# An attention and feed-forward kernel on one core: GpSimd ordered behind VectorE by semaphores, one more batch in 64-row bursts, and a new order of work

## The chip, the cores and the metric

The kernel runs on one core of a Trainium2 chip. The metric is the device time in microseconds (us) of one execution. The kernel before took 301.77 us in the median of three runs (301.6 to 303.27).

A core has five engines with a queue of instructions each: TensorE (PE in the profile) for matrix products, VectorE (DVE), ScalarE (ACT), GpSimd (POOL), and SyncE (SP), which here only issues transfers. TensorE writes its products to PSUM, eight banks of 128 partitions by 512 fp32 numbers. VectorE and ScalarE read PSUM and SBUF; GpSimd here works on SBUF alone. An engine works its queue in order, and waits for another engine by a semaphore.

## What is computed

```python
B, H, S, D, M = 8, 8, 576, 64, 128          # batch, heads, tokens, head size, features
q_s, k_s = q * D**-0.25, k * D**-0.25
phi(x) = exp(x @ omega.T - |x|^2/2 - rowmax) / sqrt(M)
kv = sum_s phi(k)[s, m] * v[s, d]           # per batch and head: 128 x 64
z  = sum_s phi(k)[s, m]
attn = (phi(q) @ kv) / (phi(q) @ z + 1e-6)
x = attn, heads side by side                # 4608 tokens x 512
h = x @ w_in                                # 512 x 2048
g = h * clip(h + 3, 0, 6) / 6
out = g @ w_out                             # 2048 x 512, fp32 out
```

Factors that are the same in numerator and denominator drop out, so that the kernel needs of `phi(q)` only an exponential, and of `phi(k)` an exponential divided by its row's maximum (`mx`, and its reciprocal `cc`), which is multiplied into v (`vc`).

## The kernel before

**Stages.** Attention is done batch by batch (0 to 7), and one stage behind it the feed-forward part block by block: 512 tokens of a batch are a block, and the 64 tokens left over of each of the eight batches form the ninth (block 8). In a stage of some 30 us the engines share the attention of batch b, the first product (`mm1`) of block b-1 and the second product (`P0` to `P6`) of block b-2.

**Attention.** The rows of q and k come in transposed (`kT`, `qT`), 18 chunks of 128 columns that hold two 64-row halves each. They are projected on omega (`burst`, or `e_K` at line 840 and `project` at line 860). Batches 0 to 2 use the second way: a matmul of 128 rows and 256 columns for each of 18 k chunks, and two matmuls of 512 columns for each four q chunks, where half of omega's rows are zeros. Batches 3 to 7 use bursts (`ROWS = 3`): four bursts, `R.0` with six chunks and `R.1` to `R.3` with four each, in which the two 64-row halves of the array work side by side (lines 796 and 799). A burst of four chunks fills four PSUM banks, and `R.0` six, at once. ScalarE takes the exponential of each bank (lines 815, 824, or 847, 864), VectorE the maximum (820 or 851). For each of four pairs of heads (`pair`), `vc` (line 970; GpSimd, or eight small ScalarE instructions at 972) and `vcc` (977, 978) scale v, `vcl` (886, 889) does so for the left-over tokens, then TensorE forms `kv` (986, 988) and `num` (1014), and VectorE divides (`rec`, `div`; 1026, 1030). A transposing transfer from SP's queue brings the result to `xT`.

**Feed-forward.** The first product is plain (`mm1`, line 1083) or, for half of the columns from block 2 on and all of them from block 7 on, in seven products instead of eight (`mm1_quad`, line 1248): its sums of weights and inputs (`W`, `X1` to `X4`) are made at line 1343, and it holds four banks X, Y, Z, W. In a quad, `q3` copies W to the SBUF tile `p7`, and `q5` (line 1276) adds Z and `p7` back into bank W, which stays taken until the two instructions of the activation, `qr2` on ScalarE and `qg2` on VectorE (1284, 1286), have read it. The second product of blocks 1 to 8 is in seven products as well (`P0` to `P6`, line 1415); its sums `S1` to `S4` over the activations are again made by `combine` at line 1343, by GpSimd or VectorE.

**What sets the order.** `ORDER` lists every operation by its number, engine by engine; these lists are the order in each queue, and decide which engine does what. `schedule` runs through them with costs written beside each operation (its `occ`, `lat`, `issue`), only to give out PSUM banks and to note which operation must wait for which; `emit` writes the instructions and semaphore waits. Operations with a `port` (GpSimd's arithmetic, and VectorE's `combine` and `vc`) are kept apart in that model by `shared`, but no wait is written for it.

```python
                if e in o.port:
                    shared[0] = o.end - (0.07 if e == "POOL" else 0.0)
```

Loads: batch 0 comes as fp32 by SP and ScalarE; later q and k are cast on the way by GpSimd's queue, and v comes by SP's. From batch 3 on the loads wait for marks in the first product (`("m1", b - 2, 2)` and so on).

Of the kernel before, what the change touches and what calls it, by code (L numbers as in the profile page):

```python
# [16 lines left out]
EV0 = (("ACT","DVE"), ("ACT","DVE"), ("POOL", "ACT"), {"k": ("POOL", "ACT", "DVE"), "q": ("POOL", "ACT","DVE")})  # L17
# [4 lines left out]
        14, 121, 115, 117, 131, 138, 159, 147, 119, 141, 150, 144, 156, 135, 127, 153, 123, 125, 176, 129, 133, 174,  # L22
        166, 170, 172, 168, 188, 190, 203, 162, 178, 205, 164, 218, 193, 180, 220, 233, 208, 195, 235, 210, 407, 248,
        395, 223, 401, 198, 396, 238, 402, 397, 240, 408, 403, 398, 245, 225, 409, 404, 410, 213, 413, 416, 243, 228,
        271, 419, 291, 251, 422, 425, 428, 431, 275, 281, 434, 277, 437, 279, 318, 440, 443, 273, 309, 446, 315, 306,
        289, 285, 449, 312, 287, 297, 300, 586, 596, 303, 326, 320, 597, 336, 576, 294, 587, 330, 577, 588, 328, 283,
        578, 598, 332, 324, 589, 322, 599, 357, 579, 566, 359, 567, 362, 344, 580, 590, 568, 346, 334, 383, 569, 570,
        571, 349, 370, 385, 591, 365, 572, 581, 375, 372, 388, 600, 601, 592, 582, 583, 352, 391, 593, 573, 378, 602,
        603, 617, 505, 620, 614, 623, 466, 469, 475, 478, 635, 490, 472, 629, 632, 487, 481, 647, 484, 659, 644, 507,
        501, 653, 638, 497, 493, 668, 503, 499, 665, 662, 495, 650, 779, 511, 509, 531, 519, 780, 521, 536, 533, 524,  # L30
        789, 555, 782, 783, 560, 557, 790, 543, 712, 545, 548, 792, 793, 692, 795, 798, 799, 705, 796, 816, 810, 813,
        719, 819, 825, 828, 840, 831, 834, 845, 842, 844, 802, 863, 847, 803, 868, 849, 851, 865, 744, 870, 867, 732,
        987, 874, 737, 997, 734, 988, 872, 768, 756, 746, 1003, 749, 761, 990, 758, 998, 773, 770, 991, 1000, 1001, 900,
        1004, 1006, 1007, 913, 1018, 1024, 1021, 920, 1010, 1027, 1033, 927, 1039, 1050, 1048, 1036, 1011, 1042, 1053,
        1071, 1052, 1073, 1055, 1076, 1057, 1075, 952, 1059, 1078, 1080, 1195, 940, 976, 1082, 942, 957, 1196, 945, 954,
        1205, 964, 1198, 969, 966, 1199, 1206, 978, 981, 1121, 1208, 1209, 1108, 1214, 1215, 1128, 1229, 1232, 1226,
        1241, 1135, 1235, 1244, 1256, 1247, 1250, 1261, 1258, 1260, 1211, 1263, 1279, 1212, 1265, 1284, 1267, 1283,
        1281, 1218, 1286, 1403, 1404, 1290, 1148, 1160, 1219, 1150, 1165, 1288, 1184, 1162, 1153, 1406, 1413, 1414,
        1329, 1189, 1407, 1186, 1172, 1416, 1174, 1177, 1336, 1417, 1419, 1420, 1316, 1422, 1423, 1440, 1437, 1434,
        1452, 1464, 1449, 1443, 1466, 1468, 1469, 1458, 1455, 1471, 1426, 1473, 1427, 1343, 1475, 1487, 1356, 1611,  # L40
        1491, 1492, 1358, 1380, 1489, 1361, 1494, 1382, 1368, 1612, 1370, 1498, 1496, 1373, 1614, 1392, 1621, 1615,
        1622, 1537, 1394, 1397, 1385, 1624, 1625, 1544, 1627, 1628, 1551, 1630, 1634, 1631, 1524, 1635, 1642, 1645,
        1672, 1648, 1651, 1657, 1660, 1677, 1674, 1676, 1663, 1564, 1576, 1679, 1566, 1578, 1569, 1666, 1681, 1695,
        1581, 1683, 1588, 1699, 1600, 1590, 1697, 1593, 1700, 1722, 1702, 1602, 1723, 1605, 1704, 1706, 1753, 1732,
        1725, 1776, 1726, 1733, 1757, 1758, 1755, 1781, 1735, 1760, 1736, 1762, 1764, 1778, 1780, 1783, 1741, 1799,
        1742, 1787, 1785, 1738, 1804, 1801, 1824, 1803, 1806, 1822, 1739, 1808, 1810, 1826, 1827, 1745, 1876, 1829,
        1746, 1831, 1833, 1878, 1845, 1881, 1880, 1901, 1846, 1883, 1899, 1885, 1848, 1904, 1903, 1849, 1887, 1924,
        1906, 1922, 1908, 1855, 1927, 1926, 1856, 1910, 1929, 1945, 1858, 1931, 1949, 1933, 1950, 1859, 1861, 1947,
        1862, 1952, 1864, 1978, 1865, 1956, 1968, 1969, 1868, 1869, 1954, 1979, 1984, 1971, 1981, 1982, 1985, 1972,
        1988, 1989, 1997, 2003, 2000,  # L50
    ],
    "SP": [
        0, 18, 22, 33, 20, 23, 26, 25, 24, 27, 28, 32, 29, 30, 31, 262, 260, 261, 465, 464, 462, 463, 461, 459, 460,
# [72 lines left out]
        1390, 1462, 1485, 1619, 1463, 1509, 1640, 1638, 1641, 1560, 1575, 1559, 1574, 1562, 1654, 1402, 1587, 1586,  # L126
        1598, 1656, 1655, 1669, 1692, 1670, 1749, 1715, 1874, 1728, 1717, 1671, 1694, 1731, 1730, 1729, 1796, 1872,
        1797, 1873, 1819, 1875, 1774, 1844, 1821, 1843, 1896, 1898, 1851, 1897, 1775, 1919, 1853, 1852, 1921, 1854,
        1944, 1965, 1976,
    ],  # L130
}

# [288 lines left out]
def _emit(nc, es, q, k, v, omega, w_in, w_out, out):  # L421
# [803 lines left out]
    def mm1_quad(blk, f):  # L1225
# [11 lines left out]
        def bank(v):  # L1237
            return v.ring.t[v.slot]
# [373 lines left out]
```

## Time and profile before

| what | before |
|---|---|
| median of three runs | 301.77 us |
| the profiled execution | 302.46 us, span 300.6 us |
| TensorE busy | 292.2 us, 97% of the span, 2899 matmuls |
| VectorE busy | 271.4 us, 90% |
| ScalarE busy | 212.9 us, 71% |
| GpSimd busy | 206.3 us, 69% |
| granted TensorE clock | 1.000 |
| share of the last chain on TensorE | 81% |

The span runs from the first to the last instruction; the 1.86 us between it and the execution's time lie around it. A matmul's busy time overlaps the next one's, so that 97% is not a share of useful work: the distance from one start to the next is the measure. That distance is 109 ns for 256 columns and 216 ns for 512 whenever nothing is waited for. In the views, `L1415` and the like are lines of the kernel before, and `x8` counts merged instructions.

### The profile page before, as it was taken

What the parts mean: (1) busy time and instruction counts of PE and PEld (TensorE: products, weight loads), DVE (VectorE), ACT (ScalarE), POOL (GpSimd) and SP (SyncE); (2) the same over time, 40 slices, a digit from 0 to 9 for tenths busy, and PEclk for the clock granted to TensorE, in tenths of its full rate; (3) what the DMA queues carried; (4) which work ended last, traced back from release to release, by engine and by line L of the source; (5) the groups of instructions that cost most, each with busy time, mean ns of one, the idle gap of its engine ahead of it and who ended that gap; (6) DMA issues with size and microseconds to landing.
All of it is one profiled execution on the core that took longest, in us unless ns stands there. A gap on an engine that the chain in (4) does not pass through costs nothing.

```text
span 300.6 us, 7551 instructions
## 1 busy us (share of the span) xinstructions
PE 292.2 (97%) x2899; PEld 222.1 (74%) x2899; DVE 271.4 (90%) x593; ACT 212.9 (71%) x479; POOL 206.3 (69%) x226
## 2 busy tenths in 40 slices
PE   7999999999999999999989999999999999999996
PEld 5688955554884798569736887588757788888885
DVE  4889898889999998999879998999999999997875
ACT  2975899199878992997587776985887576687310
POOL 1664827039898986589939869998279939869711
PEclk9999999999999999999999999999999999999999
DMA  7999999999999997799769898999531600300034
GB/s 234 292 188 168 266 200 127 197 215 155 242 110 234 126 191 138 173 139 196 171 169 172 144 241 129 106 200 220 86 94 57 166 0 3 126 16 0 2 143 140
DMA packets 90100, 44.90 MB, mean 149 GB/s; under 512 B 57936, under 2 KB 87760, under 8 KB 90064
## 3 DMA queue, kind: packets, MB, share of 16 engines
q1 hardware_dynamic: 62064, 30.71, 46.1%
q0 software_dynamic: 26592, 12.46, 33.7%
q10 hardware_dynamic: 1408, 1.25, 1.3%
q8 instruction: 23, 0.38, 0.5%
q14 instruction: 13, 0.11, 0.1%
HBM read 36.73 MB, written 9.44 MB: 154 GB/s over the span
## 4 chain that ended last, share of the span: by engine, by line
PE 81%; DVE 8%; ACT 5%; POOL 5%; issue 1%; POOLq 0%
PE p L1415 29%; PE p L1248 15%; PE p L1083 11%; PE p L1327 5%; PE p L1302 4%; PE p L1014 3%; PE p L986 2%; DVE mx L820 2%; PE p L796 2%; POOL s L1343 2%; PE p L597 2%; ACT kp L847 2%; PE p L860 2%; POOL vc L970 1%; PE p L840 1%; PE p L799 1%
## 5 line engine op out<-in xcount | busy, mean ns | idle before, releaser
L1284 ACT ACTIVATE tsb<-p 128x512 f16<-128x512 f32 x72 | 41.4, 601 | 21.8 <-PE p L1248 12.0
L1083 PE MATMUL p<-xT,wi 128*128 128x512 f16 x224 | 53.1, 379 | 1.8 <-ACT qpT L824 1.4
L1286 DVE SCALAR_TENSOR_TENSOR gT<-tsb,p 128x512 f16<-128x512 f16 x72 | 46.8, 676 | 3.0 <-ACT tsb L1284 2.8
L1415 PE MATMUL p<-wo,gT 128*128 128x256 f16 x368 | 47.0, 273 | 0.0
L1083 PEld LDWEIGHTS p<-xT,wi 128*128 128x128 f16 x224 | 21.3, 98 | 24.9 <-ACT qpT L824 2.1
L1091 DVE SCALAR_TENSOR_TENSOR gT<-tsb,p 128x512 f16<-128x512 f16 x56 | 36.4, 674 | 3.1 <-ACT tsb L1089 2.8
L1415 PEld LDWEIGHTS p<-wo,gT 128*128 128x128 f16 x368 | 34.8, 98 | 4.9 <-issue 0.5
L1089 ACT ACTIVATE tsb<-p 128x512 f16<-128x512 f32 x56 | 33.2, 620 | 7.0 <-PE p L1083 5.3
L543 ACT COPY p<-p 128x512 f32<-128x512 f32 x55 | 32.2, 599 | 4.1 <-PE p L1415 2.0
L970 POOL TENSOR_TENSOR vc<-v,cc 128x512 bf16<-128x512 f32 x27 | 28.7, 1061 | 7.1 <-DVE cc L964 5.2
L824 ACT ACTIVATE qpT<-p 128x512 bf16<-128x512 f32 (+1 forms) x50 | 27.7, 577 | 6.8 <-PE p L799 6.8
L1343 POOL TENSOR_TENSOR gT<-gT,s 128x512 f16<-128x512 f16 x21 | 24.3, 1157 | 12.0 <-PE p L1415 10.6
L1415 PE MATMUL p<-t,gT 128*128 128x256 f16 x256 | 31.8, 273 | 0.4 <-DVE u L1431 0.4
L1343 POOL TENSOR_TENSOR gT<-gT 128x512 f16<-128x512 f16 x24 | 28.2, 1177 | 4.7 <-DVE s L1343 3.2
L815 ACT ACTIVATE kp<-p 128x512 bf16<-128x512 f32 (+1 forms) x50 | 26.8, 571 | 5.9 <-PE p L799 5.6
L820 DVE TENSOR_REDUCE mx<-kp 128x4 f32<-128x512 bf16 (+1 forms) x50 | 29.3, 618 | 0.3 <-ACT kp L815 0.3
L643 POOL DMA_DIRECT2D kb<-in_k_dram x21 | 16.2, 774 | 18.8 <-PE p L1083 18.1
L1030 DVE TENSOR_TENSOR xb<-p,rec 128x384 f16<-128x384 f32 (+1 forms) x64 | 28.2, 467 | 0.3
L1415 PEld LDWEIGHTS p<-t,gT 128*128 128x128 f16 x256 | 24.3, 98 | 5.4 <-issue 1.3
L1343 POOL TENSOR_TENSOR s<-gT,s 128x512 f16<-128x512 f16 x21 | 24.4, 1164 | 3.4 <-DVE s L1343 2.2
L1343 POOL TENSOR_TENSOR s<-gT 128x512 f16<-128x512 f16 x19 | 22.0, 1158 | 4.7 <-DVE gT L1286 3.1
L643 POOL DMA_DIRECT2D qb<-in_q_dram x28 | 19.6, 713 | 7.5 <-PE p L1083 5.0
(139 smaller groups left out, 671.4 us busy)
## 6 DMA issues: line engine op xcount, KB each, us to landing
v<-in_v_dram SPq DMA_DIRECT2D x14, 512.0 KB, 4.8
out_dram<-osb SPq DMA_DIRECT2D x14, 512.0 KB, 3.3
kb<-in_k_dram POOLq DMA_DIRECT2D x14, 256.0 KB, 5.0
qb<-in_q_dram POOLq DMA_DIRECT2D x14, 256.0 KB, 5.6
wo<-in_moe_w_out_dram POOLq DMA_DIRECT2D x8, 256.0 KB, 9.9
wi<-in_moe_w_in_dram POOLq DMA_DIRECT2D x3, 512.0 KB, 7.5
q<-in_q_dram SPq DMA_DIRECT2D x4, 256.0 KB, 4.8
vl<-in_v_dram SPq DMA_DIRECT2D x8, 128.0 KB, 4.2
```

The source lines that it names most:

```text
L543: return E.copy(dst(), src())
L643: lambda E: E.dma_start(dst, src), prio + 0.001 * turn_of[0], reads=gate, writes=keys,
L820: op("DVE", dvet(128 * (d1 - d0)), lambda E, ko=ko, mo=mo: E.reduce_max(mo, ko, axis=AX.X), p0 + 0.01, reads=[("kp", 0, d, lh) for d in ra ...
L970: return E.tensor_tensor(vcm[:, :, 0:D], v32[:, m, :, :], cbc, ALU.mult)
L1083: ins = E.matmul(ring.t[vh.slot], wi[:, c, 128 * f:128 * f + 128], xv[:, c, :], start=(c == 0), stop=(c == NJ - 1))
L1089: op("ACT", actt(512), lambda E: E.activation(tsb[tu][:], ring.t[vh.slot], AF.Relu, bias=0.5, scale=1.0 / 6.0), t - 0.1, reads=[vh], write ...
L1091: op("DVE", dvet(512), lambda E: E.scalar_tensor_tensor(gT[gu][:, f, :], tsb[tu][:], 1.0, ring.t[vh.slot], ALU.min, ALU.mult), t - 0.1, re ...
L1248: ins = E.matmul(bank(v)[:, 256 * g:256 * g + 256], w(c, f + g), x[:, c, :], start=start and g == 0 and c == 0, stop=c == 1, skip_group_ch ...
L1284: op("ACT", actt(512), lambda E, v=v, tu=tu: E.activation(tsb[tu][:], bank(v), AF.Relu, bias=0.5, scale=1.0 / 6.0), t - 0.1, reads=[v], wr ...
L1286: op("DVE", dvet(512), lambda E, v=v, tu=tu, dst=dst: E.scalar_tensor_tensor(dst, pieces(tsb[tu][:]), 1.0, pieces(bank(v)), ALU.min, ALU.m ...
L1343: op(engines, {"POOL": 0.1 + n / 475.0, "DVE": 0.09 + n / 2000.0}, lambda E: E.tensor_tensor(dst, x, y, ALU.subtract if minus else ALU.add ...
L1415: ins = E.matmul(ring.t[v.slot][:, 256 * j:256 * j + 256], a[:, f, 128 * j:128 * j + 128], w[:, f, :], start=(first and f == 0 and j == 0) ...
```

## The change

Three things are done together, and all five lists of `ORDER` are new.

1. **GpSimd waits for VectorE.** `schedule` remembers the last VectorE operation with a `port` (`holder`), and lets each following `port` operation of GpSimd depend on it, if by the model less than 4 us lie between. `emit` makes a semaphore wait of it where no other wait covers it. `qg2` of each quad joins these VectorE operations, since `q5` now writes its sum to `p7` in SBUF in place of bank W: `qr2` and `qg2` then read SBUF, and bank W is free once `q3` has copied it.
2. **Bursts from batch 2.** `ROWS` goes from 3 to 2: the third batch's 9 `K` and 10 `Q` operations become `R2.0` to `R2.3`.
3. **A new sequence.** TensorE's queue has 546 operations for 561, ScalarE's 456 for 442, VectorE's 592 for 593, GpSimd's 215 for 222; SP's 112 for 112. `vc` of batch 0 is cut in two halves by v's two loads. Loads from batch 3 on have no marks to wait for. Many costs in the model are other numbers; they emit nothing, and act only through bank choice and through `holder`.

By names, the parts of the lists that matter below: `vc.0.1` is `vc` of batch 0, pair 1, and a second operation of one name has a mark ('); `wi` and `wo` are loads of the weights, `kl.1` and `k10.1` loads of batch 1, `Tevk` and `Tevq` copies of transposed k and q out of PSUM, `eK` and `eQ` the exponentials. GpSimd at the start, before: `wi1 wi0 wi0' wi2 vcl.0 vc.0.0 vc.0.1 vcc.0.2 vc.0.2 vc.0.3 kl.1 wi3 k00.1`; after: `wi1 wi0 wi0' vc.0.0 vc.0.0' vcl.0' vcl.0 vc.0.1' wi2 wi3 kl.1 vcc.0.3 k10.1`. ScalarE between `eK0.6` and its first `eQ`, before: `vcl.0' eQ0.0A eK0.7 Tevq0.l vcc.0.0`; after: `Tevq0.0A vcc.0.0 Tevq0.1A Tevq0.l eQ0.0A'`. TensorE around the third batch, after: `mm1.1.0 .8 .1 .2 .9 R2.1 mm1.1.10 mm2.0.1 mm2.0.1 mm1.1.3 R2.3 mm1.1.4 .11 .12 R2.2 mm1.1.13 .5 .6 P1.0 R2.0 mm1.1.7`. In the stage of batch 5, before: `R5.0 P3.5 P3.5' R5.2 mm1.4.8 .1 .0 .2 R5.3`; after: `R5.0 P3.5 P3.5' R5.2 R5.3 mm1.4.1`. At block 8's end, before: `qc.8.6 P8.2' P8.4`; after: `qc.8.6 P7.6 P8.4 P7.6' P8.2 P8.2'`, and the sums of block 8 are 2 on GpSimd for 8. Over all blocks GpSimd has 81 of the `S` sums for 85, 13 of the `X` sums for 14, none of the copies `Swv` for 3, and `vcl` 15 for 13.

```diff
--- before.py
+++ after.py
@@ -14,119 +14,117 @@
-EV0 = (("ACT","DVE"), ("ACT","DVE"), ("POOL", "ACT"), {"k": ("POOL", "ACT", "DVE"), "q": ("POOL", "ACT","DVE")})
+EV0 = (("ACT","DVE"), ("ACT","DVE"), ("POOL", "ACT", "DVE"), {"k": ("POOL", "ACT", "DVE"), "q": ("POOL", "ACT","DVE")})
...
@@ -217,6 +215,7 @@
         shared = [0.0]
+        holder = None
         queues = {}
@@ -328,7 +327,11 @@
                 if e in o.port:
-                    shared[0] = o.end - (0.07 if e == "POOL" else 0.0)
+                    shared[0] = o.end - (0.08 if e == "POOL" else -0.15)
+                    if e == "DVE":
+                        holder = o
+                    elif holder is not None and st - holder.end < 4.0:
+                        o.deps.setdefault(holder, False)
             for vx in o.virts:
@@ -435,7 +438,7 @@
     SPLIT = 3
-    ROWS = 3
+    ROWS = 2
     BURSTS = [[(0, 2), (2, 6)], [(6, 10)], [(10, 14)], [(14, 18)]]
@@ -641,8 +644,8 @@
                lambda E: E.dma_start(dst, src), prio + 0.001 * turn_of[0], reads=gate, writes=keys,
-               group="d" + part + ("c" if cast else "") + (str(pb) if b and part != "v" else ""), inc=16, lat=LANDS.get(part, 1.5) if b == 0 else 1.8 if b == 1 else 1.2,
-               name="%s.%d" % (part, b), issue=0.76 if cast else 0.62 if b else 0.52, packet=50.0 if run == 1024 else 18.0)
+               group="d" + part + ("c" if cast else "") + (str(pb) if b and part != "v" else ""), inc=16, lat=LANDS.get(part, 1.5) if b == 0 else 1.6,
+               name="%s.%d" % (part, b), issue=(0.63 if part[1] == "l" and part[0] == "q" else 0.77) if cast else 0.62 if b else 0.53, packet=50.0 if run == 1024 else 18.0)
             turn_of[0] += 1
...
@@ -963,18 +966,25 @@
            reads=[("mx", pb, d, h) for d in dbls for h in range(2)], writes=[("cc", pb, m)], name="cc" + nm)
-        cbc = bass.AP(cc[pb], c0, [[NCH, 128], [1, 8], [0, D]])
+        def cbc(i0, i1):
+            return bass.AP(cc[pb], c0 + i0, [[NCH, 128], [1, i1 - i0], [0, D]])
+
         vcm = vc[u2][:].rearrange("p (c e) -> p c e", e=65)
-        def e_vc(E):
-            if E is not nc.scalar:
-                return E.tensor_tensor(vcm[:, :, 0:D], v32[:, m, :, :], cbc, ALU.mult)
-            for i in range(8):
-                ins = E.activation(vcm[:, i, 0:D], v32[:, m, i, :], AF.Copy, scale=cc[pb][:, c0 + i:c0 + i + 1])
-            return ins
-
-        op(EV_VC if b else V0, {"POOL": 1.08, "DVE": dvet(512), "ACT": 1.88}, e_vc, t, port=("POOL", "DVE"), reads=[("cc", pb, m), ("v32", 0, m), ("v32", 1, m)], writes=[("vc", u2, 0)], name="vc" + nm)
+        for hs in ([0], [1]) if b == 0 else ([0, 1],):
+            i0, i1 = 4 * hs[0], 4 * hs[-1] + 4
+
+            def e_vc(E, i0=i0, i1=i1):
+                if E is not nc.scalar:
+                    return E.tensor_tensor(vcm[:, i0:i1, 0:D], v32[:, m, i0:i1, :], cbc(i0, i1), ALU.mult)
+                for i in range(i0, i1):
+                    ins = E.activation(vcm[:, i, 0:D], v32[:, m, i, :], AF.Copy, scale=cc[pb][:, c0 + i:c0 + i + 1])
+                return ins
+
+            n = 64 * (i1 - i0)
+            op(EV_VC if b else V0, {"POOL": 0.125 + n / 512.0, "DVE": dvet(n), "ACT": 0.24 * (i1 - i0)}, e_vc, t, port=("POOL", "DVE"),
+               reads=[("cc", pb, m)] + [("v32", hh, m) for hh in hs], writes=[("vc", u2, 2 * hh) for hh in hs], name="vc" + nm)
         ccr = cc[pb][:, c0:c0 + 8].rearrange("p (r o) -> p r o", o=1)
-        op(EV_L, {"ACT": 0.1, "POOL": 0.18}, lambda E: E.copy(vcm[:, :, D:D + 1], ccr) if E is nc.scalar
+        op(EV_L, {"ACT": 0.1, "POOL": 0.31}, lambda E: E.copy(vcm[:, :, D:D + 1], ccr) if E is nc.scalar
            else E.tensor_tensor(vcm[:, :, D:D + 1], ones[:].rearrange("p (r o) -> p r o", o=1), ccr, ALU.mult), t, port="POOL",
@@ -987,8 +997,8 @@
 
-        op("PE", 8 * 0.03 + 0.06, e_kv, t, reads=[("kp", 0, d, h) for d in [m // 2] + list(dbls) for h in range(2)] +
-           [("vc", u2, i) for i in range(2)] + [("vcl", pb, i) for i in range(2)],
+        op("PE", 0.315, e_kv, t, reads=[("kp", 0, d, h) for d in [m // 2] + list(dbls) for h in range(2)] +
+           [("vc", u2, i) for i in range(3)] + [("vcl", pb, i) for i in range(2)],
            writes=[vkv], alloc=[vkv], lat=0.25, slack=sl, spare=sp, name="kv" + nm)
...
@@ -1235,7 +1245,7 @@
         def bank(v):
-            return v.ring.t[v.slot]
+            return v.ring.t[v.slot] if isinstance(v, Virt) else p7[v[1]][:]
 
@@ -1273,11 +1283,11 @@
         op("PE", each, four(Y, orig(1, 1), X4s[u]), t + STEP[2], reads=[("X4", u)] + khi, writes=[Y], lat=0.25, name="qc." + nm)
-        op("DVE", dvet(512), lambda E: E.tensor_tensor(bank(W), bank(Z), p7[w7][:], ALU.add), t - 0.1, reads=[("p7", w7), Z], writes=[W],
-           name="q5." + nm)
+        op("DVE", dvet(512), lambda E: E.tensor_tensor(p7[w7][:], bank(Z), p7[w7][:], ALU.add), t - 0.1, reads=[Z],
+           writes=[("p7", w7)], name="q5." + nm)
         op("PE", each, four(Z, summed(W4s), b[1][1]), t + STEP[2], reads=["W4%d" % h] + xkeys(blk, 1, 1), writes=[Z, at(3)], lat=0.25,
            name="qd." + nm)
-        for n, (v, i, k_) in enumerate(((X, 0, 0), (Y, 1, 0), (W, 1, 1), (Z, 0, 1))):
+        for n, (v, i, k_) in enumerate(((X, 0, 0), (Y, 1, 0), (("p7", w7), 1, 1), (Z, 0, 1))):
             tu = hcount[0] % 3
@@ -1285,7 +1295,8 @@
                 dst, pieces(tsb[tu][:]), 1.0, pieces(bank(v)), ALU.min, ALU.mult),
-               t - 0.1, reads=[v, ("t", tu)], writes=[("gT", gu, 8 * i + f + x, k_) for x in range(2)], name="qg%d.%s" % (n, nm))
+               t - 0.1, reads=[v, ("t", tu)], writes=[("gT", gu, 8 * i + f + x, k_) for x in range(2)], name="qg%d.%s" % (n, nm),
+               port="DVE" if n == 2 else ())
 
...
@@ -1554,7 +1565,7 @@
         else:
-            load(b, (), {"k": [("m1", b - 2, 2)], "q": [("m1", b - 2, 4)], "v": [("m1", b - 2, 9)]})
+            load(b, (), {t: [] for t in "kqv"})
         if b == 0:
@@ -1566,6 +1577,9 @@
                     mm1_half(half, f)
+            for h in range(2):
+                if FIRST7[h] == 1:
+                    input_sums(h)
             continue
```

## The prediction

> **What bounds the kernel now.** First the page's busy shares and its last chain, then the busy time by stretches.
>
> ```profile
> PE 292.2 (97%) x2899; PEld 222.1 (74%) x2899; DVE 271.4 (90%) x593; ACT 212.9 (71%) x479; POOL 206.3 (69%) x226
> PE 81%; DVE 8%; ACT 5%; POOL 5%; issue 1%; POOLq 0%
> ...
> 0.00:25.00 25.00, 22.66 (x233) 17.89 (x234) 17.81 (x59) 16.05 (x38) 13.90 (x25) 1.00 1.09 233
> 150.00:175.00 25.00, 23.15 (x218) 16.04 (x216) 23.22 (x48) 20.07 (x49) 17.82 (x21) 1.00 1.00 163
> ```
>
> TensorE (first number after the stretch) lacks time in the first 25 us and in 150 to 175, almost nowhere else. Going through its starts in the timeline, with 109 ns for 256 columns and 216 for 512, I find after 28 us these waits: 1.4 us at 151, 0.6 at 160, 0.2 at 166, 0.1 at 208, 0.8 at 237, 0.6 at 280, 0.3 at 94: 4.1 us. From 12 to 28 us another 1.5 us of waits and 18 filler matmuls of 0.109 us (line 597), 3.5 us together. All else is work at full pace, so only fewer matmuls, or these 7.6 us, can make it faster.
>
> The chain of waits shows who is late at 150 to 160, the timelines what happens at 280 (GpSimd, VectorE, TensorE):
>
> ```profile
> 149.12 0.60 ACT qpT L824
> 149.72 0.98 ACT kp L815 x2
> 150.70 0.77 ACT qpT L824 x2
> 151.46 1.04 ACT kp L815 x3
> 152.93 1.04 PE p L1083 x4
> ...
> 158.41 1.25 DVE q L1343
> ```
> ```profile
> 277.69 2.38 POOL L1343 TENSOR_TENSOR gT<-gT,s 128x512 f16<-128x512 f16 x2
> 278.94 1.41 DVE L1343 TENSOR_TENSOR s<-gT,s 128x512 f16<-128x512 f16 x1
> 280.28 0.68 DVE L1431 TENSOR_TENSOR u<-p 128x512 f32<-128x512 f32 x1
> 281.01 1.05 PE L1415 MATMUL p<-t,gT 128*128 128x256 f16 x8 [0.42 <-DVE u L1431]
> ```
>
> After a burst ScalarE empties banks and TensorE waits for one; at 280 a VectorE sum takes 1.41 us while GpSimd's second sum runs to 280.07, and TensorE waits behind. The times of that sum over the run:
>
> ```profile
> L1343 DVE TENSOR_TENSOR s<-gT,s x11: 408/424/1411, 82.0 to 287.2; 128x512 f16<-128x512 f16 x11
> L1343 POOL TENSOR_TENSOR gT<-gT,s x21: 1149/1155/1216, 86.9 to 294.4; 128x512 f16<-128x512 f16 x21
> ```
>
> **What the Trainium skill says.** "SBUF — State Buffer", "Who interferes with whom": a VectorE instruction with two SBUF inputs and a GpSimd one that reads SBUF exclude each other for the whole instruction. The trace agrees at 280: 0.41 us free, 1.41 blocked. All 512-element VectorE sums together exceed 0.41 us by 8.4 us; the reverse, GpSimd over its medians of 1.16 and 1.05, comes to some 2 us. One sum does not fit: at 158.33 it took 1.33 us though GpSimd issued transfers until 159.5. "TensorEngine Tiling (Array Packing)", "Theoretical Speedup": 64 rows give up to 2x. Here it is 1.4x, below. "Perfetto Trace Analysis", "Optimization Strategy": repeated bubbles can mean too few PSUM banks; the wait at 151 is one.
>
> **The change part by part**, against the profiled span of 300.6 us; its execution took 302.46, 1.86 outside the span, 0.7 above the median. I apply the difference of spans to the median, 301.77.
>
> *Bursts.* The third batch's plain projections stand here, with bursts of a later batch:
>
> ```profile
> 62.53 1.04 PE L840 MATMUL p<-om,kT 128*128 128x256 bf16 x8
> 63.40 1.03 PE L1083 MATMUL p<-xT,wi 128*128 128x512 f16 x4
> ...
> 209.29 0.40 PE L796 MATMUL p<-om,kT 64*128 64x128 bf16 x8
> 209.53 0.38 PE L799 MATMUL p<-qT,om 64*128 64x512 bf16 x2
> 209.84 0.61 PE L1014 MATMUL p<-kvz,qpT 128*128 128x65 bf16 x14
> ```
>
> Eight k matmuls take 63.40 - 62.53 = 0.87 us. Plain: 18 x 0.109 + 8 x 0.216 + 2 x 0.109 = 3.91 us. A burst of four chunks takes 209.84 - 209.29 = 0.55, and starts 0.10 late after the matmul before it: 0.64; that of six 0.86. Three and one: 2.79. Off TensorE: 1.1 us, in a stretch without waits (59 to 78), so on the path. Against it: ScalarE is busy without a break from 60 to 77 us, issuing a 512-column instruction each 0.49 us. Its work stays (one half instruction more for k, as for VectorE's maxima), but the new order gives it nothing but five activations during `mm1.1.0 .8 .1 .2 .9` (4.3 us of TensorE, 2.4 of ScalarE), and then four banks at once. Going through the new order with 0.86 us a `mm1` and 0.49 an evacuation, I find TensorE some 0.4 us early at `R2.3`, 0.35 at `R2.0` (six of eight banks) and 0.3 at the `mm1` behind it. Net gain 0.2 to 1.1; I take 0.5. K's load is issued as late as before (behind `vc.1.2`, `vc.1.3`; before, the last k transfer left at 50.5 us and `kT` landed at 60.65), and `R2.1` comes some 63 us in: 2 us of cover. If that goes, the delay is TensorE's.
>
> *Start.* Before, the first `kv` starts at 15.62: GpSimd does `wi2`, `vcl` (12.28), then `vc.0.0` (13.00 to 14.04), and `vcc` stands on ScalarE behind a `vcl` of 1.05 us and four evacuations, until 15.34. New: both halves of `vc` first (v's loads landed at 11.93 and 12.88; half of 1.04 each, to 13.5), then two `vcl` of 0.62, to 14.9; `vcc` ahead. `kv` about 15.1, 0.5 us earlier, and ScalarE is rid of 1.05 but gets two copies of 0.59; VectorE gets five half `vc` (none shown; between 0.2 and 0.4 us each, from the 0.41 of an f16 sum of 512) for those two copies. `wi2` is issued some 4 us later than 11.49; it landed in 11 us then, and is first used near 25: no more than covered. Bounds: 1 us lost to 3.5 gained; I take 0.7.
>
> *Semaphore waits.* GpSimd's new waits follow 100 or so VectorE operations: sums, `vc`, and 18 `qg2`, which now hold the port for some 0.68 us each, 12 us that were free to GpSimd before. A wait ends 0.08 us after VectorE (sum to 221.92, GpSimd at 222.00), which is also the usual gap between two GpSimd sums: nothing where VectorE is in time. What is gained is VectorE's blocked time, of which the waits at 160 and 280 (1.2 us) and the 0.3 at 94 (a sum of 1.38 us at 88.7 ahead of it) are on the path. Taken: 1.2 us; bounds 0 and 1.5, and a loss where VectorE is late (below). Gone as well is the load's mark: GpSimd sat 18.1 us for k and 5.0 for q on it, but no waiter of TensorE stood behind.
>
> *Bank W free early, fewer copies on GpSimd.* 18 banks are free one sum and two activation steps sooner; no wait names W, so 0, between a gain of 0.5 and a loss of 0.5 if the next `q3` must wait for `p7`. GpSimd loses 4 sums, a net `X`, three `Swv` (0.79), gains two `vcl`: some 7 us less, off the path but at 237. ScalarE's 14 more operations, some 5 us, lie in its 88 us of idle time; VectorE trades sums for copies.
>
> *Sequence, the rest.* 151: `R5.2` and `R5.3` now stand together, eight banks, and `R5.3` must wait for the last of `R5.0`, which ScalarE ended at 152.5 before, against 151.6 for the end of `R5.2`: with 0.2 us on top some 1.1 us of wait in place of 1.4. 237: GpSimd has 11 operations, 12 us, from `vc.7.1` to the sum of `P6.2`, TensorE 11.3 us between: 0.7 in place of 0.8. 280: `P8.2'` now stands four products, 3.5 us, behind `qc.8.6`; counted above. SP's `vl.5` now stands ahead of a k transpose of batch 4 and must wait for `vcl.3`, which comes before `kv.3` anyway: 0. I take 0.2 gained; bounds 2.6 gained, 3 lost.
>
> Sum: 0.5 + 0.7 + 1.2 + 0.2 = 2.6; 301.77 - 2.6 = 299.2.
>
> **Rivals.** (1) *The waits are cleared.* The start gives 2 us, the bursts all 1.1, and 2.4 of the 4.1 go: 5.5 us, 296.3. For it: TensorE needs none of these waits. Against it: ScalarE's and GpSimd's lateness in a stage are work, not order. (2) *Nothing arrives.* The 1.1 us of the bursts are given back at the banks of ScalarE, VectorE's free time falls into its own idle 10%, and new small waits replace old: 301.5. For it: ScalarE's full stretch from 60 to 77. (3) *Slower: GpSimd held behind a late VectorE.* GpSimd's queue is in order; before, it went ahead when VectorE was late, now it waits, and behind it stand `vc` and the sums that `kv` and the products need. In 222 to 238 GpSimd's work runs without a break and TensorE waits 0.8 us for its end. VectorE is 90% busy with instructions of 0.6 to 0.7 us; one instruction late, it costs GpSimd 0.7. Two such waits in each of seven attention stages are 9.8 us of GpSimd's time; if its idle third absorbs half, TensorE gets 5 us: 299.2 + 5 = 304.2. It decides from 2.6 / 7 = 0.37 us a stage on, where the gain is eaten. (4) *The wait does nothing* is part of (2): a VectorE sum that comes after a running GpSimd sum is blocked as before.
>
> **Chances.** Mine 0.46 (297.5 to 300.2), the first 0.16, the second 0.17, the third 0.21. A measurement tells some 0.5%, 1.5 us, from no change: faster 0.62, same 0.17, slower 0.21. The range from 295.8 to 304.2 cuts the first and the third in half.
>
> **What would show it.** Bursts: lines 840 and 860 fewer by 18 and 10 matmuls, waits under 1.1 us between 58 and 80. Start: the first `kv` near 15.1, fewer fillers. Waits: VectorE's longest sums near 0.45, GpSimd waiting on VectorE in more places, each under 0.7. It is wrong if GpSimd's waits on VectorE are followed by TensorE's on `vc` or sums, if transposed k is late at `R2.1`, or if a burst finds its banks taken for over 1 us.

## The result and the profile after

| | before | after |
|---|---|---|
| median | 301.74 us (4 runs) | 298.48 us (4 runs) |
| span of the profiled execution | 300.6 us | 296.6 us |
| TensorE busy | 292.2 us | 290.8 us |
| VectorE busy | 271.4 us | 266.4 us |
| ScalarE busy | 212.9 us | 218.1 us |
| GpSimd busy | 206.3 us | 194.3 us |

The ratio is 0.9877 with an interval of 0.9851 to 0.9903: 3.3 us, or 1.2%, faster. 299.2 was forecast. The spans of the two profiled executions differ by 4.0 us, since that of before lies 0.7 us above its median; the terms below are made against the spans.

The page of the kernel after, in the order in which the prediction showed it: engines, chain, and the two stretches in which TensorE lacked time.

```profile
PE 290.8 (98%) x2908; PEld 220.7 (74%) x2908; DVE 266.4 (90%) x592; ACT 218.1 (74%) x487; POOL 194.3 (66%) x219
...
PE 93%; ACT 5%; DVE 1%; issue 0%
...
0.00:25.00 25.00, 23.17 (x222) 17.27 (x223) 17.38 (x57) 16.29 (x38) 13.22 (x26) 1.00 1.10 237
150.00:175.00 25.00, 24.21 (x253) 18.01 (x252) 24.69 (x57) 20.24 (x48) 19.14 (x22) 1.00 0.90 145
```

The last chain was on TensorE for 81% and is now for 93%; VectorE's 8% are 1%, GpSimd's 5% are gone. From 150 to 175 us TensorE is busy for 24.21 us where it was for 23.15. What it still waits for is a short list. Here are TensorE's waits (engine, line, what it waited for: us in all, times, longest), before and then after:

```profile
PE p L1083 <- ACT qpT L824: 1.4, 1, 1.4
PE p L1415 <- POOL s L1343: 0.7, 1, 0.7
...
PE p L1083 <- DVE gT L1091: 0.4, 1, 0.4
PE p L1415 <- DVE u L1431: 0.4, 1, 0.4
```
```profile
PE p L600 <- DVE fill L595: 1.5, 1, 1.5
PE p L799 <- ACT kp L818: 0.8, 1, 0.8
PE p L1093 <- DVE gT L1101: 0.4, 1, 0.4
```

The four of before are those at 151, 237, 160 and 280 us. After, `fill` is in the first microseconds, where it was before too; 0.8 us are in front of `R5.3` (151.55), and 0.4 behind the new burst `R2.0` (74.11). Nothing is left at 160, 237 and 280. Distances between starts, beyond those of work at full pace, give after 28 us: before 0.30 + 0.22 + 1.43 + 0.58 + 0.23 + 0.83 + 0.58 = 4.2 us (at 28, 94, 153, 160, 166, 238, 281), after 0.44 + 0.85 + 0.07 = 1.4 us (at 74, 151.55, 152.16). That is 2.8 of the 4.0 us; about 1.1 are fewer and denser matmuls, and some 0.2 are in the start.

VectorE's sums in the kernel after, by tile (smallest, median and largest ns of one):

```profile
L1354 DVE TENSOR_TENSOR gT<-gT,s x15: 393/419/1193, 87.4 to 290.0; 128x512 f16<-128x512 f16 x15
L1354 DVE TENSOR_TENSOR s<-gT,s x13: 394/418/728, 109.7 to 283.6; 128x512 f16<-128x512 f16 x13
```

Few are blocked any more: what all sums of 512 elements take beyond 0.41 us comes to 1.6 us together, against 8.4 before.

### The profile page after: what moved, and what is told of

Read it like the earlier page. It is cut to its first block, busy times and chain, and to the rows that moved or that the text cites. A ratio compares the mean times of both kernels' runs of the same rounds, so it can differ in the third digit from the quotient of the medians.

```text
span 296.6 us, 7597 instructions
## 1 busy us (share of the span) xinstructions
PE 290.8 (98%) x2908; PEld 220.7 (74%) x2908; DVE 266.4 (90%) x592; ACT 218.1 (74%) x487; POOL 194.3 (66%) x219
## 4 chain that ended last, share of the span: by engine, by line
PE 93%; ACT 5%; DVE 1%; issue 0%
PE p L1426 32%; PE p L1258 19%; PE p L1093 16%; PE p L1313 5%; PE p L1338 5%; PE p L1024 3%; PE p L996 3%; PE p L799 3%; PE p L802 2%; ACT kp L850 2%; PE p L600 1%; ACT qpT L867 1%; PE p L843 1%; ACT qpT L827 1%; ACT kp L818 1%; PE p L558 1%
## 5 line engine op out<-in xcount | busy, mean ns | idle before, releaser
L1294 ACT ACTIVATE tsb<-p 128x512 f16<-128x512 f32 x72 | 42.4, 618 | 12.3 <-PE p L1258 9.6
L1296 DVE SCALAR_TENSOR_TENSOR gT<-tsb,p 128x512 f16<-128x512 f16 x72 | 48.3, 685 | 1.3 <-ACT tsb L1294 0.8
L1101 DVE SCALAR_TENSOR_TENSOR gT<-tsb,p 128x512 f16<-128x512 f16 x56 | 36.8, 677 | 2.1 <-ACT tsb L1099 1.6
L818 ACT ACTIVATE kp<-p 128x512 bf16<-128x512 f32 (+1 forms) x60 | 31.7, 573 | 8.1 <-PE p L802 8.1
L823 DVE TENSOR_REDUCE mx<-kp 128x4 f32<-128x512 bf16 (+1 forms) x60 | 35.7, 622 | 1.8 <-ACT kp L818 1.4
L1099 ACT ACTIVATE tsb<-p 128x512 f16<-128x512 f32 x56 | 34.0, 625 | 4.4 <-PE p L1093 4.0
L827 ACT ACTIVATE qpT<-p 128x512 bf16<-128x512 f32 (+1 forms) x60 | 33.0, 584 | 5.1 <-PE p L802 4.9
L978 POOL TENSOR_TENSOR vc<-v,cc 128x512 bf16<-128x512 f32 (+1 forms) x26 | 26.0, 1000 | 5.8 <-DMA v<-in_v_dram 1.4
L1040 DVE TENSOR_TENSOR xb<-p,rec 128x256 f16<-128x256 f32 (+1 forms) x64 | 28.2, 469 | 0.2
L1354 POOL TENSOR_TENSOR s<-gT,s 128x512 f16<-128x512 f16 x19 | 21.9, 1154 | 4.3 <-DVE s L1354 2.4
L1354 POOL TENSOR_TENSOR gT<-gT,s 128x512 f16<-128x512 f16 x17 | 19.7, 1156 | 5.4 <-DVE s L1354 2.3
L1024 PEld LDWEIGHTS p<-kvz,qpT 128*128 128x128 bf16 x312 | 14.5, 98 | 3.3 <-ACT kvz L546 0.8
```

Of the source, the lines that this page charges most:

```text
L818: op("ACT", actt(128 * (d1 - d0)), lambda E, lh=lh, ko=ko, part=part: E.activation(ko, out_of(part, 0, lh)[0].rearrange("p (x m) -> p x m" ...
L823: op("DVE", dvet(128 * (d1 - d0)), lambda E, ko=ko, mo=mo: E.reduce_max(mo, ko, axis=AX.X), p0 + 0.01, reads=[("kp", 0, d, lh) for d in ra ...
L827: op("ACT", actt(128 * (d1 - d0)), lambda E, lh=lh, part=part: E.activation(qd[:, part[0]:part[1], lh, :], out_of(part, 1, lh)[0].rearrang ...
L1099: op("ACT", actt(512), lambda E: E.activation(tsb[tu][:], ring.t[vh.slot], AF.Relu, bias=0.5, scale=1.0 / 6.0), t - 0.1, reads=[vh], write ...
L1101: op("DVE", dvet(512), lambda E: E.scalar_tensor_tensor(gT[gu][:, f, :], tsb[tu][:], 1.0, ring.t[vh.slot], ALU.min, ALU.mult), t - 0.1, re ...
L1294: op("ACT", actt(512), lambda E, v=v, tu=tu: E.activation(tsb[tu][:], bank(v), AF.Relu, bias=0.5, scale=1.0 / 6.0), t - 0.1, reads=[v], wr ...
```

## Experiments

Each kernel was run in turn with the kernel before, on one chip; ratios are to before, and in brackets is the 95% interval. The changed kernel has 0.9877 [0.9851, 0.9903]; it was not run again beside them, so a difference from it goes through the two ratios. Each kernel left one profile, so that a wait at a named place is seen in one execution.

### What the waits are worth

**The changed kernel without the waits.** All else stays: sequence, bursts, `q5` into `p7`.

```diff
-                    elif holder is not None and st - holder.end < 4.0:
-                        o.deps.setdefault(holder, False)
```

> The changed kernel without the new waits: the two lines that let a GpSimd operation depend on the last two-SBUF-input operation of VectorE are left out, order and bank choice stay. Theory W (the waits give what the prediction gave them, 1.2 us, by sparing VectorE its blocked sums): VectorE's 512-element sums exceed their free 0.41 us by 5 us or more in total again (1.3 in the changed kernel), TensorE waits for a late VectorE, and the time is 299.3 to 300.5 (298.5 with the waits). Theory S (the new sequence alone gives the gain, the waits only cost nothing): 298.0 to 298.8. Theory C (the waits cost time that the sequence hides): under 298.

303.36 us, ratio 1.0045 [1.0029, 1.0062]: slower than the kernel before, and outside the ranges of all three theories. VectorE's sums and activations in this kernel, the last chain, some of TensorE's waits, and the sum at 174.90 with what GpSimd did then:

```profile
L1352 DVE TENSOR_TENSOR s<-gT,s x13: 390/417/1728, 110.7 to 288.2; 128x512 f16<-128x512 f16 x13
L1294 DVE SCALAR_TENSOR_TENSOR gT<-tsb,p x72: 630/677/1577, 103.6 to 288.9; 128x512 f16<-128x512 f16 x72
```
```profile
PE 82%; DVE 10%; ACT 5%; issue 1%; DVEq 0%
```
```profile
PE p L1256 <- DVE p L1284: 1.1, 2, 0.9
...
PE p L1424 <- DVE osb L1440: 0.6, 1, 0.6
PE p L1424 <- DVE s L1352: 0.5, 1, 0.5
```
```profile
174.90 1.73 DVE L1352 TENSOR_TENSOR s<-gT,s 128x512 f16<-128x512 f16 x1
...
174.34 0.81 POOL L644 DMA_DIRECT2D kb<-in_k_dram  x1
175.16 2.47 POOL L1352 TENSOR_TENSOR gT<-gT 128x512 f16<-128x512 f16 x2
...
176.68 1.05 PE L1424 MATMUL p<-t,s 128*128 128x256 f16 x8 [0.48 <-DVE s L1352]
```

Medians are as before, the largest are not: the sums exceed 0.41 us by 10.0 us together, the 18 `qg2` their median of 0.68 by 2.0, GpSimd's sums theirs by 4.2. What theory W named is what happens, in a larger size. VectorE's sum at 174.90 ends 0.3 us after GpSimd's first one (175.16 to 176.33), and TensorE, whose `P` product reads that sum, waits for it. There are six waits of TensorE on VectorE that the changed kernel doesn't have: 0.80 us at 100.9, 0.34 at 156.1, 0.64 at 176.7, 0.40 at 210.9, 1.08 at 250.5, 0.32 at 260.3, together 3.6 of the 4.7 us between the two spans (301.3 and 296.6).

**The same waits alone, in the kernel before.** The lines above added to it, nothing else; `qg2` stays out, since there it reads PSUM.

> The kernel before with the new waits alone: the same rule for a dependence, its own order. Theory W: VectorE's sums lose most of their 8.4 us of blocked time, the waits of TensorE at 160 and 280 go, and the time is 300.3 to 300.9 (301.7 before). Theory S: 301.4 to 302.0. The rival of the prediction that GpSimd is held behind a late VectorE: over 302.5, with TensorE's wait near 237 longer than 0.8 us, since the order was not made for the waits.

300.92 us, ratio 0.996 [0.9946, 0.9973]: 1.2 us faster. The waits at 160 and 280 are gone, those at 151 (0.81) and 237 (0.82) stay. Sums are still blocked:

```profile
L1348 DVE TENSOR_TENSOR s<-gT,s x11: 408/424/1202, 82.4 to 285.5; 128x512 f16<-128x512 f16 x11
```

Their excess falls from 8.4 only to 5.7 us. The lines add 13 semaphore waits of GpSimd on VectorE here (56 before, 69 here), and nearly as many in the changed kernel (64 without them, 78 with them), where the excess falls from 10.0 to 1.6 us. Why they spare less here is not shown.

**`qg2` out of the operations that GpSimd waits for**, in the changed kernel.

```diff
-               port="DVE" if n == 2 else ())
+               port=())
```

> The changed kernel in which the third activation of a quad (qg2, now with two SBUF inputs) no longer counts among the operations that GpSimd waits for; sums and vc still do. If the lock between qg2 and GpSimd matters (18 instructions of 0.68 us): VectorE's qg2 run up to 1 us longer than 0.68 in several places and the time is 0.3 to 1 us above the changed kernel's 298.5. If the sums' waits alone carry it: 298.2 to 298.8.

300.75 us, ratio 0.9955 [0.9941, 0.997], 2.3 us slower than the changed kernel and more than was expected. `qg2` itself grows little (up to 1334 ns, 1035 in the changed kernel). What grows are GpSimd's and VectorE's sums: their excess is 2.6 and 4.2 us (0.4 and 1.6 in the changed kernel). At 170.85 a GpSimd sum takes 1.61 us beside a `qg2`, the next one 1.38, and then VectorE's sum at 174.42 takes 1.72. TensorE waits 0.63 us behind it, at 176.2, and 0.32 at 258.9. A further 0.97 us, at 153.07, is not clearly due to the edit: `mm1.4.1` starts there 0.09 us after a transposing transfer of x landed, which here took 5.8 us for 4.9. That leaves about 1.3 us for `qg2`.

**The wait made mutual.** VectorE's `port` operations also depend on GpSimd's last one.

```diff
-                    if e == "DVE":
-                        holder = o
-                    elif holder is not None and st - holder.end < 4.0:
-                        o.deps.setdefault(holder, False)
+                    last = holders.get("POOL" if e == "DVE" else "DVE")
+                    if last is not None and st - last.end < 4.0:
+                        o.deps.setdefault(last, False)
+                    holders[e] = o
```

> The changed kernel, with the wait made mutual: a VectorE operation with a port also depends on the last GpSimd operation with a port, if by the model less than 4 us lie between. Theory 1, GpSimd's wait acts because it keeps GpSimd from starting ahead of VectorE's turn; the other direction is then settled as well, VectorE only waits where it would have been blocked: the same within 0.4 us, 298.1 to 298.9, with VectorE's sums at 0.41 us. Theory 2, waits as such cost time at each handing over (0.08 us from one engine's end to the other's start, and a late GpSimd now holds all of VectorE's queue, not one instruction): 1 us or more slower than the changed kernel, 299.5 to 301.

298.63 us, ratio 0.9889 [0.9865, 0.9913]: the same. The sums by tile:

```profile
L1354 DVE TENSOR_TENSOR gT<-gT,s x15: 395/418/426, 87.2 to 289.6; 128x512 f16<-128x512 f16 x15
L1354 DVE TENSOR_TENSOR s<-gT,s x13: 392/418/427, 109.6 to 283.3; 128x512 f16<-128x512 f16 x13
```

No sum is blocked at all, and it brings nothing. That VectorE's last blocked time was covered by its idle time is the likely reading, and the handing over has no price here that a run can tell.

**`q5` into `p7` alone, in the kernel before**, gave no kernel, so that no run separates this step from the new order. In the lists of before, `q5` must then stand behind `q4`, and `schedule` stops at `qd.2.6`: on TensorE `qd.2.6` waits for `q5.2.6`, which on VectorE stands behind `rec.3.0B`, which waits for `num.3.0B`, which on TensorE stands behind `qd.2.6`. The changed order with bank W was not tried.

### The bursts

**The third batch's projections plain**, in the changed kernel: `ROWS = 3`, each burst's operations in its place.

```diff
-    ROWS = 2
+    ROWS = 3
```

> The changed kernel with the third batch's projections plain again: each burst of batch 2 is replaced in TensorE's list by its plain projections in one go, ScalarE's and VectorE's by the answering instructions. Prediction: the bursts are worth 0.2 to 1.1 us, 0.5 taken: 298.7 to 299.6. By the profile of after (1.1 us less work, 0.44 us of new wait behind R2.0): 0.65, so 299.1. If the bursts only gave their time back to ScalarE: 298.4 to 298.6. If the smaller banks' steps suit ScalarE better than bursts: under 298.4.

299.44 us, ratio 0.9917 [0.9896, 0.9939]: 0.4% slower than the changed kernel, with an uncertainty of nearly the same size. The traces are sharper. From the `mm1` at 57.89 to the first `kv` at 77.58 the changed kernel needs 19.69 us; plain, 58.16 to 78.51, 20.35. That is 0.66 us. Without the bursts' own wait of 0.44 it would be 1.1. First the two ends in the changed kernel, with that wait between them, then the two ends in the plain one:

```profile
57.89 4.48 PE L1093 MATMUL p<-xT,wi 128*128 128x512 f16 x20
...
73.13 0.39 PE L799 MATMUL p<-om,kT 64*128 64x128 bf16 x8
73.36 0.38 PE L802 MATMUL p<-qT,om 64*128 64x512 bf16 x2
74.11 2.76 PE L1093 MATMUL p<-xT,wi 128*128 128x512 f16 x12 [0.38 <-DVE gT L1101]
...
77.58 0.42 PE L996 MATMUL p<-vc,kp 128*128 128x65 bf16 x8
```
```profile
58.16 4.48 PE L990 MATMUL p<-xT,wi 128*128 128x512 f16 x20
...
78.51 0.42 PE L893 MATMUL p<-vc,kp 128*128 128x65 bf16 x8
```

**`R2.0` one `mm1` later** (`P1.0 mm1.1.7 R2.0` for `P1.0 R2.0 mm1.1.7` on TensorE), first on TensorE alone, then with that `mm1`'s `relu` and `g` moved ahead of the burst's evacuations as well.

> The changed kernel, with the third batch's first burst R2.0 one mm1 later (P1.0, mm1.1.7, R2.0 in place of P1.0, R2.0, mm1.1.7). The changed kernel's trace has 0.44 us of wait on TensorE behind R2.0 (74.1 us). Theory 1, the place in the order is what costs: the burst takes its six banks too early, 0.86 us later they are there, the wait goes and nothing takes its place; 0.4 us faster than the changed kernel, 298.1 us. Theory 2, ScalarE's and VectorE's work behind the bursts is what is late: the wait moves to R2.0 itself or to P1.2 and kv.2.1 behind it, and the time stays within 0.2 us of 298.5.

> The changed kernel, with R2.0 one mm1 later on TensorE and the two steps of that mm1's activation (relu.1.7 on ScalarE, g.1.7 on VectorE) moved ahead of R2.0's exponentials and maxima as well. R2.0 one mm1 later on TensorE alone was 0.5% slower than the changed kernel: mm1.1.7's activation still stood behind R2.0's exponentials. Theory 1, order: with the other two queues moved too, the banks are free when R2.0 wants them and the 0.44 us behind it go: 298.1 us. Theory 2, ScalarE works without a break here and every place costs the same: 298.3 to 298.8 us, with waits of the same sum between 58 and 80 us.

299.77 us, 0.9931 [0.991, 0.9951], and 299.93 us, 0.9934 [0.991, 0.9958]: both 0.5% slower than the changed kernel, which is outside the second theories' ranges too. TensorE's waits from 58 to 80 us are 0.44 us in the changed kernel, 2.0 in the first and 1.2 in the second. In the first, `mm1.1.7`'s activation stands behind the exponentials of a burst that now comes later. In the second, TensorE still waits in front of `R2.0` (0.35) and behind it (0.37), and then twice for `kv` (0.45 at 78.9, 0.42 at 81.2), probably since `R2.0` is what the pairs' maxima hang on. Theory 1 falls: of the three places tried, the one with the 0.44 us is the cheapest.

### The wait at 151 us

**`R5.3` three operations later**, and, in another kernel, **`R5.0` and `R5.2` ahead of their two products each**.

```diff
- R5.0 P3.5 P3.5' R5.2 R5.3 mm1.4.1 qa.4.4 mm1.4.0
+ R5.0 P3.5 P3.5' R5.2 mm1.4.1 qa.4.4 R5.3 mm1.4.0
```
```diff
- num.4.3A P3.3 P3.3' R5.0 P3.5 P3.5' R5.2 R5.3
+ num.4.3A R5.0 P3.3 P3.3' R5.2 P3.5 P3.5' R5.3
```

> The changed kernel, with the burst R5.3 three operations later, behind mm1.4.1 and qa.4.4 (1.3 us of TensorE's work). The changed kernel waits 0.85 us in front of R5.3 (150.4 to 151.6) and 0.27 us behind it. Theory 1, order: two bursts side by side ask for eight banks at once; with 1.3 us of other work between them the wait is gone, and so are 0.8 us or more: 297.6 us. Theory 2, ScalarE's work: it issues exponentials without a break in this stretch, mm1.4.1 and qa.4.4 need banks too and wait for the same instructions; at most 0.3 us is gained: 298.2 to 298.8.

> The changed kernel, with R5.0 in front of P3.3 and R5.2 in front of P3.5 (before: each behind its two products, some 1.8 us). ScalarE stood idle for 0.74 us at 148.3 until R5.0 was there, and TensorE then waited 0.85 us in front of R5.3. Theory 1, the wait is ScalarE's lateness, and it is late because it gets its work late: R5.0 1.7 us earlier fills ScalarE's gap, the wait in front of R5.3 falls from 0.85 to about 0.1 us, and the time to 297.7 us. Theory 2, eight banks: R5.0's six banks are not free 1.7 us earlier, TensorE waits in front of R5.0 instead; 298.3 to 299.5 us.

299.63 us, 0.9933 [0.9909, 0.9956], and 300.74 us, 0.9958 [0.9944, 0.9971]: slower, both, and by more than any of their theories had it. In the second, TensorE waits 1.47 us in front of `R5.0` for a bank, which is what its theory 2 named. The first shows something that I had not looked for. TensorE, behind `R5.2`:

```profile
151.64 1.04 PE L990 MATMUL p<-xT,wi 128*128 128x512 f16 x4 [1.10 <-DMA xT<-xb]
```

`mm1.4.1` waits for a transfer: the last of four that bring batch 4's result, transposed, to `xT`. It was issued at 146.99 and landed at 151.59. The same look at the other traces, with the last transfer's issue, its landing, and the start of the first `mm1` on it:

| kernel | issued | landed | first `mm1` |
|---|---|---|---|
| before | 148.24 | 152.84 | 152.93 |
| before, with the waits | 148.38 | 152.39 | 152.48 |
| after | 147.22 | 152.07 | 152.16 |
| before, without marks (below) | 147.54 | 150.03 | 151.37, no wait |

So in the kernel before the wait at 151 is this transfer's. The view named ScalarE, whose instruction ended at about the same time (152.79). But the program lets this `mm1` (there `mm1.4.8`) wait for another instruction of ScalarE, the exponential `eQ5.2.0`, and for the four transfers; that exponential had ended at 151.19. In the kernel with `R5.3` later, TensorE waits once more behind this place, 0.69 us at 154.35 for ScalarE.

**The kernel before without the loads' marks.**

```diff
-            load(b, (), {"k": [("m1", b - 2, 2)], "q": [("m1", b - 2, 4)], "v": [("m1", b - 2, 9)]})
+            load(b, (), {t: [] for t in "kqv"})
```

> The kernel before, with the loads of batches 3 to 7 free of their marks in the first product; nothing else. GpSimd waited 18.1 us for k's marks and 5.0 us for q's in the kernel before. Theory 1, no waiter of TensorE stands behind these waits, the loads leave earlier but are not needed earlier: 301.5 to 302.5 us, as before, TensorE's waits at 151, 160, 237 and 280 unchanged. Theory 2, GpSimd's sums behind the loads come earlier and with them what TensorE waits for at 237 and 280: 0.5 to 1.5 us faster, 300.5 to 301.5 us. Theory 3, without the marks GpSimd's sums now meet VectorE's at other times and block them more: 303 us or more.

301.32 us, ratio 0.9979 [0.9963, 0.9994]: 0.6 us faster, at the lower end of theory 2. Of the two waits that theory 2 named, the one at 280 is gone in the trace and the one at 237 stays (0.80); the one at 151 is gone too, and TensorE waits 0.33 us at 161 and 0.27 at 164 instead. The profiled execution was 1.0 us faster than the median of its runs, so that not every wait that is missing in it needs to be the marks' doing. Here is the end of the transfers of x, before and without marks (launch of the last two; their times to landing):

```profile
L1059 SPq DMA_TRANSPOSE xT<-xb x2: 1254/1332/1410, 146.8 to 148.2; - x2
...
DMA to landing us min/median/max: 2.5/3.6/4.6
```
```profile
L1059 SPq DMA_TRANSPOSE xT<-xb x2: 1256/1260/1265, 146.2 to 147.5; - x2
...
DMA to landing us min/median/max: 2.5/2.5/2.5
```

With 2.5 us for the last one TensorE doesn't wait, with 4.6 it waits 1.4 us, in the same order of TensorE and ScalarE. So ScalarE's work and the banks are not what costs there.

**`R5.3` later, and batch 5's second v load 8 us earlier on SP's queue**, so that it doesn't follow the last transfer of x.

```diff
- v00.5 Xdma.4.0 Xdma.4.1 Xdma.4.2 Xdma.4.3 v10.5
+ v00.5 v10.5 Xdma.4.0 Xdma.4.1 Xdma.4.2 Xdma.4.3
```

> The changed kernel, with R5.3 behind mm1.4.1 and qa.4.4 as in one run above, and on SP's queue batch 5's second v load right behind the first (issued some 8 us earlier, near 140.3 us), so that it no longer follows the last transposing transfer of x. In the traces mm1.4.1 starts 0.05 to 0.1 us after that transfer lands, and it landed 4.0 to 5.8 us after its issue in the runs that wait there, 2.5 us in the run without marks, which doesn't wait. Theory 1, the transfer of x is what is late, because v's bytes are moved beside its own: it now lands 2.5 us after its issue, near 150 us, mm1.4.1 follows R5.2 at once, R5.3 finds its banks free behind it, and the waits between 145 and 162 fall from the changed kernel's 1.8 to about 0.8 us: 297.5 to 298.0 us. Theory 2, v's bytes aren't the cause: x lands as late as before, and the time is that of R5.3 moved alone, 299.6 us. Theory 3, x comes early, but ScalarE's banks then hold R5.3 or what follows as long: 298.3 to 299.2 us.

300.48 us, ratio 0.994 [0.9917, 0.9963]. Theory 1 falls. The ratio can't be told from that of `R5.3` later alone (0.9933), as theory 2 had it. All four transfers of x now take 5.0 to 8.4 us, the last 6.0, and TensorE waits longer than ever (this profiled execution took 2.1 us more than the median of its runs; the names in it count, not its length):

```profile
153.38 1.87 PE L990 MATMUL p<-xT,wi 128*128 128x512 f16 x4 [2.49 <-DMA xT<-xb]
```

That the first `mm1` waits for x's transfer is shown. A v load behind it isn't what makes the last one late, or not alone: the run without marks has that load behind it too (1.3 us later, as in before). The traces of all fourteen profiled kernels point elsewhere. A transfer lands in 16 parts, and 15 of them land within 0.2 us of each other. In eleven traces the sixteenth comes 1.5 to 2.8 us after these, 4.0 to 6.0 us after the issue. In each of the eleven a 16 KB packet of the queue that the DMA view calls "instruction" started 2.0 to 2.9 us before that sixteenth part landed (in the kernel before at 150.84; 15 parts were in at 150.71, the last at 152.84). In the other three (without marks, `R5.0` and `R5.2` earlier, third batch plain) all 16 parts land 2.5 to 2.9 us after the issue, and the packet comes only after that. Packet and lateness go together without an exception; no run moved the packet, so that it is the cause is not shown.

### The start

**`vc` of batch 0 whole**, in the changed kernel, in the places of the halves (pair 0 on GpSimd, the others on VectorE).

```diff
-        for hs in ([0], [1]) if b == 0 else ([0, 1],):
+        for hs in ([0, 1],):
```

> The changed kernel, with vc of batch 0 whole, as before the change: pair 0 on GpSimd in the place of its second half, pair 1 on VectorE in the place of its first half, pairs 2 and 3 on VectorE. Theory 1, the halves are worth what the place of v's loads gives: the first half lies under the wait for v's second load, so a whole vc ends 0.42 us later (1.04 against 0.62 us from 13.24 us on), the first kv starts near 15.8 instead of 15.39 us, pair 1 saves GpSimd 0.75 us: 298.5 to 299.0 us. Theory 2, the start is bound elsewhere (maxima on VectorE, vcc): first kv at 15.4, 298.1 to 298.5 us.

298.59 us, ratio 0.991 [0.9878, 0.9942]: no difference from the changed kernel that can be told. GpSimd's `vc` in the changed kernel, and here:

```profile
12.27 0.61 POOL L978 TENSOR_TENSOR vc<-v,cc 128x256 bf16<-128x256 f32 x1 [1.01 <-DMA v<-in_v_dram]
13.24 0.62 POOL L978 TENSOR_TENSOR vc<-v,cc 128x256 bf16<-128x256 f32 x1 [0.36 <-DMA v<-in_v_dram]
```
```profile
12.61 1.04 POOL L875 TENSOR_TENSOR vc<-v,cc 128x512 bf16<-128x512 f32 x1 [1.48 <-DMA v<-in_v_dram]
```

The first `kv` in the two:

```profile
15.39 0.42 PE L996 MATMUL p<-vc,kp 128*128 128x65 bf16 x8
```
```profile
15.69 0.42 PE L893 MATMUL p<-vc,kp 128*128 128x65 bf16 x8
```

Half a `vc` takes 0.61 us, 0.59 of a whole one, and the second half waits for v again. Here both loads were in at 12.6, so that the whole `vc` ended sooner (13.65 for 13.86). The first `kv` still came 0.3 us later (15.69 for 15.39), the second only 0.1 (16.44 for 16.33), and nothing is left at the end.

## Why the prediction was right, and where it was not

The time is within 0.7 us of the forecast, in part by luck: the sum hides two errors of opposite sign (the start 0.5 too much, the sequence 1.7 too little) and one wrong cause. Term by term, against the spans:

- **Bursts: 0.5 taken, 0.66 measured.** The 1.1 us off TensorE came out (20.35 - 19.69 + 0.44). Three places were named where ScalarE gives time back, with 1.05 us; one does, behind `R2.0`, with 0.44. Lines 840 and 860 have the forecast 18 and 10 matmuls fewer, k was not late at `R2.1`, and no burst found its banks taken for over 1 us in this stretch.
- **Start: 0.7 taken, 0.2 measured.** The first `kv` starts at 15.39, not 15.1 (15.62 before). The step that failed is "v's loads landed at 11.93 and 12.88; half of 1.04 each, to 13.5": in the kernel after, these loads landed at 12.12 and 13.11, so that the second half had to wait 0.36 us, and a half takes 0.62 us, not 0.52. The second half ended at 13.86. VectorE's half `vc` takes 0.42 us where 0.2 to 0.4 were forecast. From 5 to 28 us the fillers fell from 3.05 to 2.07 us, but TensorE's waits rose from about 1.7 to 2.5.
- **Semaphore waits: 1.2 taken, 1.4 measured** (0.58 at 160, 0.58 at 281, 0.22 at 94), and 1.2 when they alone are added to the kernel before. The mechanism is right. But that term is the waits' worth *in the kernel before*. In the changed one they are worth 4.9 us (303.36 - 298.48), since all its other changes together make it 0.45% slower than before. 2.3 of the 4.9 us come only when GpSimd waits for `qg2` as well. The prediction counted the 12 us for which `qg2` now holds the port, and gave them no price in case the waits weren't there. The loads' marks, which it costed at nothing, are worth 0.6 us in the kernel before.
- **Bank W, fewer copies on GpSimd: 0 taken.** No run separates it. TensorE has no wait for W in the changed kernel. GpSimd's busy time fell by 12 us where some 7 were forecast, and its last arithmetic ends at 273.4 us (295.5 before).
- **Sequence, the rest: 0.2 taken, 1.9 measured** (151: 0.5; 237: 0.83; 166: 0.23; 28: 0.30). This is the term that was mis-sized, within its bound of 2.6. For 237 the count of GpSimd's 11 operations gave 0.7 us of wait; there is none. Adding the waits alone left it (0.82), taking the marks away left it (0.80), and even the changed kernel without waits has none there. What is left is the sequence, with `q5` into `p7`. For 151 "after a burst ScalarE empties banks and TensorE waits for one" was wrong for the kernel before: x's transfer was late. The Trainium skill, "Perfetto Trace Analysis", "Optimization Strategy", takes a gap that repeats over a stretch as a possible sign of too few buffers; the wait at 151 stands once, and was no such case. For the kernel after, `R5.3` does wait for banks, 0.85 us where 1.1 were forecast, and the transfer of x, landing at 152.07, would have held `mm1.4.1` until 152.16 without that wait. The two causes end within 0.6 us (151.49 for the bank, 152.07 for the transfer), so that taking away the first alone could gain next to nothing; `R5.3` later was even slower.

The third rival, GpSimd held behind a late VectorE, did not come. GpSimd does wait for VectorE, and longer than "each under 0.7": the list of GpSimd's waits after has single ones of 11.1, 5.4 and 3.1 us. But these are mostly waits for results that GpSimd needs: without the new lines the list has 11.1, 5.9 and 7.6, and all of GpSimd's waits on VectorE add up to 47.2 us without them and 52.7 with them. No wait of TensorE on GpSimd is left. GpSimd's idle third, now 34%, takes them all. The first rival (296.3) asked for 2.4 of the 4.1 us of waits; 2.8 came. What kept the time from it are the start, which gave 0.2 instead of 2 us, and the 0.44 of the bursts.

## What to carry to other kernels

What an ordering wait between two engines that block each other is worth depends on the kernel around it: here the same lines were worth 0.4% in the kernel before, and 1.7% in the changed one, which has another order and 18 more VectorE instructions with two SBUF inputs. Some 0.8 of the 1.7% hang on these 18; how much is the order's own is not shown. So test such a wait in the kernel that it was made for, with and without it. Where a wait in front of a product ends, look up which instructions and transfers the program lets it wait for, and compare its end with theirs, before you believe the engine that the view names. Where two causes end close together, taking away one gains little.

## What the hardware showed that was not expected

- VectorE's sum at 174.90 in the run without waits started 0.26 us before GpSimd's and still took 1.73 us. By the Trainium skill, "SBUF — State Buffer", "Who interferes with whom", the instruction that issues first has the ports. GpSimd was issuing a transfer until 175.15 then. The sum at 98.56 is alike (0.18 us ahead, 1.64 us). But in the same run the sums at 88.84, 123.06 and 153.17, also 0.09 to 0.25 us ahead of GpSimd's and beside the issue of a transfer, took 0.39 to 0.42 us. And the sum at 158.33 of the kernel before took 1.33 us though GpSimd had only transfers to issue until 159.5. What sets these apart stays open.
- A `scalar_tensor_tensor` with two SBUF inputs is blocked as sums are: without the waits three of the 18 `qg2` took 1.04, 1.33 and 1.58 us beside GpSimd's arithmetic, for a median of 0.68. The other 54 activations of that line, with one input in PSUM, took at most 0.69.
- A transposing transfer of the same size landed 2.4 to 8.4 us after its issue. The last of batch 4's was late by one of its 16 parts, in just those traces in which a packet of the instruction queue came between.
